# A fused attention and Mish kernel: two more buffers for first-layer results, softmax weights in PSUM, and a new order of steps

## The chip, the core and the metric

The kernel runs on one core of a Trainium2 chip. Its time is the device time in microseconds (us) of one execution; the median of a few executions is quoted. Five engines work side by side, each through its own queue of instructions in a fixed order, and wait for each other through semaphores: TensorE (PE, matrix products, with results in PSUM), VectorE (DVE), ScalarE (ACT), GpSimd (POOL) and SyncE (SP, which here issues the DMA transfers). PSUM has eight banks of 512 fp32 columns by 128 partitions.

## The reference

All inputs are fp32, with S = 2048 rows, D = 640, H = 32 heads of Dh = 20, windows of W = 8 keys with a stride of 2, and F = 1728.

```
x = A_x
g = sigmoid((x * gate_w).sum(-1, keepdims=True))
# a: sliding, dilated, causal attention
q, k, v = split_heads(x @ wqkv)
logits[h, s, w] = q[h, s] . k[h, s - 2 * w] * Dh ** -0.5     # -1e9 where s - 2 * w < 0
o[h, s] = sum_w softmax_w(logits)[h, s, w] * v[h, s - 2 * w]
a = merge_heads(o) @ wo
# b: Dense, Mish, Dense
h = x @ w1 + b1
b = (h * tanh(softplus(h))) @ w2
out = g * a + (1 - g) * b
```

## The kernel before

Every fp32 product is made of three matmuls on split numbers: an operand is cut into a high part (ACT copies it rounded, L444) and a low part (DVE or POOL subtracts, L447), and `mm3` (L510 to L514) multiplies high by high, high by low and low by high into one PSUM group. Halves of the products are combined so that fewer products are needed, at the price of additions of inputs and of partial sums.

The work comes in steps with names. `u.n.i` is group i of a unit n of the projection x @ wqkv (eight units; 0 to 3 are for the first half of the rows, 4 to 7 for the second). Units 2 and 3 are made together: `p.2.j.a1` to `p.2.j.c3` (j = 0 to 3) are the steps of the pair. `q.P.n` is a block of the MLP's first layer (P = 0: half of the rows, in the form with fewer products; P = 1: the same for the other half), in the groups `first`, `second`, `m1` to `m4`, `l1`, `l2`.

In a block `q.0.n`, a group's partial sum is carried on: `seed` (L1144) is an ACT copy from one PSUM bank into the next one or into an `hb` buffer in SBUF, and the next group adds to it. `added` (L1162) is a DVE add of a bank to the kept sum in an `hb` buffer; it also empties the bank. Then `acted` (L1150) is Mish on ACT. First-layer results wait in `hb` buffers, of which there are six, until they are combined (L1017, DVE or POOL) and stored by DMA.

In the pair of units, `c1` (L876 to L882) takes a bank of ring "sb", ACT copies a kept sum into it (L879), PE adds six matmuls, and DVE makes a difference (`sum_to`, L826) in a bank of ring "qb". Then `c2` adds to the first bank and `c3` to the second; both wait for that DVE operation (`self.seeded`), and the results go to the next unit by way of ACT (L680 to L684).

The attention runs on DVE between these operations. For two slots of rows at a time: ACT copies q into `qg` in PSUM (L575), DVE multiplies q by the window of keys (L569, 2560 elements a partition) and reduces (L572) to the logits `lg`. For four slots: DVE takes the maximum `mx` (L590) and subtracts it (L591), ACT takes the exponential (L592) and writes it, multiplied by the gate, into `pw` in SBUF (L596, four pieces), and DVE sums, inverts and multiplies `pw` into `pg` in PSUM (L603 to L605). Then come the products with v (L614, L618).

There are three PSUM banks in a ring "qb", three in a ring "sb", and two that the attention's `pg` and `qg` share. A planner goes through the steps named in a table `ORDER`, adds the other engines' work by costs and ranks, and so fixes the order of the instructions on every engine. What an engine does next is then fixed; the waits decide when.

Of the kernel before, what the change touches and what calls it, by code (L numbers as in the profile page):

```python
# [253 lines left out]
ORDER = """
u.0.5 u.0.7 u.0.4 last.0 u.0.6 q.0.0.first pieces.0.1 q.0.0.m1 q.0.1.first wq.1 pieces.0.2 q.0.1.second q.0.0.second q.0.0.m3 q.0.0.m4 q.0.1.m1 last.1
q.0.0.l2 q.0.0.l1 q.0.0.m2 q.0.1.m3 sum q.0.1.m4 u.1.1 u.1.7 u.1.0 u.1.3 q.0.1.l1 q.0.1.l2 u.1.2 q.0.1.m2 u.1.4 u.1.5 q.0.2.first q.0.2.m1 u.1.6
q.0.2.second q.0.2.m3 q.0.2.m2 wa.2 q.0.2.m4 p.2.1.a1 pieces.0.3 p.2.0.a1 sum p.2.0.a2 q.0.2.l2 p.2.0.a3 p.2.0.b1 p.2.1.a2 q.0.2.l1 p.2.1.a3 p.2.0.b2
p.2.2.a1 p.2.2.a2 p.2.2.a3 p.2.2.b1 p.2.3.a1 p.2.1.b2 p.2.2.b2 p.2.3.a2 pieces.0.4 p.2.1.b1 p.2.3.a3 p.2.3.b1 p.2.3.b2 q.0.3.first q.0.3.m1
q.0.3.second q.0.3.m3 q.0.3.m2 q.0.3.m4 wc.2 q.0.4.second q.0.3.l1 p.2.0.c0 q.0.4.first q.0.3.l2 p.2.1.c0 q.0.4.m1 q.0.4.m3 q.0.4.m4 q.0.4.m2 q.0.4.l2
pieces.0.5 q.0.5.first q.0.4.l1 p.2.3.c0 q.0.5.m1 q.0.5.m4 q.0.5.second x.3.3 q.0.5.m2 x.2.1 x.3.0 p.2.0.c1 p.2.1.c1 x.3.4 p.2.0.c2 q.0.5.m3 p.2.3.c1  # L260
p.2.2.c0 p.2.2.c1 q.0.5.l1 p.2.3.c2 x.2.2 p.2.3.c3 x.3.2 x.2.3 p.2.2.c3 p.2.2.c2 x.3.1 p.2.0.c3 p.2.1.c3 p.2.1.c2 x.2.4 q.0.5.l2 wq.4 x.2.0 third sum
u.4.1 u.4.3 rest.0 pieces.1.0 u.4.5 sum u.4.0 q.1.0.m2 q.1.0.second u.4.6 u.4.2 u.4.4 u.4.7 sum rest.1 wq.5 sum q.1.0.m1 q.1.0.first u.5.0 pieces.1.1
u.5.1 pieces.1.2 sum u.5.4 u.5.2 u.5.7 wq.6 pieces.1.3 u.5.3 q.1.2.second u.5.5 q.1.1.m2 q.1.1.m1 u.5.6 q.1.1.second u.6.6 u.6.4 sum lastw.1 u.6.7
u.6.5 q.1.1.first q.1.2.m2 u.6.2 u.6.1 pieces.1.4 q.1.2.first q.1.3.m1 sum wq.7 u.6.3 q.1.2.m1 pieces.1.5 q.1.3.m2 q.1.3.second u.6.0 q.1.3.first
q.1.4.first last.2 q.1.4.m2 q.1.4.m1 q.1.4.second q.1.5.second u.7.7 u.7.4 u.7.5 last.3 q.1.5.m2 q.1.5.m1 u.7.0 q.1.5.first u.7.6 u.7.1 u.7.2 u.7.3
rest.2 rest.3
# [1696 lines left out]
```

## Time and profile before

| | |
|---|---|
| median of 3 runs | 620.61 us (620.59 to 622.07) |
| profiled execution | 620.5 us, of which the span of the profile is 618.7 us |
| PE busy | 612.1 us, 99% |
| DVE busy | 582.6 us, 94% |
| ACT busy | 364.8 us, 59% |
| POOL busy | 312.2 us, 50% |

The span runs from the first to the last instruction that the profiler saw; 1.8 us of the execution lie around it. Busy shares are means over the whole span. A matmul's shown duration includes its way through the array, so that the pace is read from start to start. Rows of the timeline show an instruction's start and its duration, and in brackets how long its engine had been idle before it and what ended that.

### The profile page before, as it was taken

The numbers are of one execution on the slowest core, as the hardware profiler recorded it, in microseconds if no ns is written. First come the engines' busy times: TensorE is split into PE (matmuls) and PEld (weight loads), VectorE is DVE, ScalarE is ACT, GpSimd is POOL, SyncE is SP. The second block draws the span as 40 slices with busy tenths as digits, with TensorE's granted clock in tenths as the row PEclk, the third lists the DMA queues.
The fourth block names the chain that finished last, engine by engine and source line by source line (L and its number), as shares of the span: only waits on it lengthen the run. The fifth ranks groups of instructions, "written<-read, shape, count | busy, mean of one in ns | idle before, by whom it ended". The sixth has DMA issues, their size and how long they took to land.

```text
span 618.7 us, 9150 instructions
## 1 busy us (share of the span) xinstructions
PE 612.1 (99%) x2719; PEld 508.5 (82%) x2719; DVE 582.6 (94%) x550; ACT 364.8 (59%) x854; POOL 312.2 (50%) x287
## 2 busy tenths in 40 slices
...
GB/s 321 226 223 114 234 251 145 269 240 313 314 297 220 195 256 275 262 250 187 221 228 344 223 123 279 282 204 276 268 242 249 245 175 184 255 275 289 275 89 119
DMA packets 100769, 145.95 MB, mean 236 GB/s; under 512 B 11552, under 2 KB 54560, under 8 KB 100496
## 3 DMA queue, kind: packets, MB, share of 16 engines
...
q8 instruction: 21, 0.34, 0.2%
...
q14 instruction: 28, 0.23, 0.1%
...
## 4 chain that ended last, share of the span: by engine, by line
PE 98%; DMA 0%; DVE 0%; ACT 0%; issue 0%; SPq 0%; DVEq 0%
PE qb L513 20%; PE qb L512 20%; PE qb L514 20%; PE sb L512 12%; PE sb L513 12%; PE sb L514 12%; PE qb L674 1%; DMA raw<-in_wq 0%; PE sb L518 0%; PE qb L519 0%; PE sb L519 0%; PE qb L518 0%; PE sb L674 0%; DVE pair L1740 0%; ACT hb L1150 0%
## 5 line engine op out<-in xcount | busy, mean ns | idle before, releaser
L447 POOL TENSOR_TENSOR pair<-raw,pair 128x512 fp32r<-128x512 f32 (+4 forms) x127 | 156.3, 1250 | 106.4 <-ACT pair L444 61.9
L513 PE MATMUL qb<-pair 128*128 128x512 f32 (+1 forms) x451 | 174.5, 387 | 0.0
L512 PE MATMUL qb<-pair 128*128 128x512 f32 (+1 forms) x451 | 174.5, 387 | 0.0
L514 PE MATMUL qb<-pair 128*128 128x512 f32 (+1 forms) x451 | 174.5, 387 | 0.0
L444 ACT ACTIVATE pair<-raw 128x512 fp32r<-128x512 f32 (+2 forms) x229 | 133.7, 608 | 61.1 <-DMA raw<-actt 19.4
L512 PE MATMUL sb<-pair 128*128 128x512 f32 (+2 forms) x326 | 126.2, 387 | 1.8 <-ACT sb L879 1.8
L513 PE MATMUL sb<-pair 128*128 128x512 f32 (+2 forms) x326 | 126.0, 387 | 0.0
L514 PE MATMUL sb<-pair 128*128 128x512 f32 (+2 forms) x326 | 126.0, 387 | 0.0
L512 PEld LDWEIGHTS qb<-pair 128*128 128x128 f32 x451 | 84.7, 188 | 16.7
L513 PEld LDWEIGHTS qb<-pair 128*128 128x128 f32 x451 | 84.7, 188 | 16.6
L514 PEld LDWEIGHTS qb<-pair 128*128 128x128 f32 x451 | 84.7, 188 | 16.5
L614 DVE TENSOR_TENSOR pr<-kvq,pg 128x1280 f32<-128x1280 f32 x64 | 93.5, 1483 | 0.9
L569 DVE TENSOR_TENSOR pr<-kvq,qg 128x2560 f32<-128x2560 f32 x32 | 89.9, 2809 | 2.0 <-ACT qg L575 0.5
L618 DVE TENSOR_REDUCE kvq<-pr 128x320 f32<-128x2560 f32 x32 | 90.2, 2818 | 0.9
L572 DVE TENSOR_REDUCE lg<-pr 128x128 f32<-128x2560 f32 x32 | 90.2, 2817 | 0.8
L447 DVE TENSOR_TENSOR pair<-raw,pair 128x512 fp32r<-128x512 f32 (+2 forms) x102 | 71.3, 720 | 3.9 <-ACT pair L444 2.3
L512 PEld LDWEIGHTS sb<-pair 128*128 128x128 f32 x326 | 61.2, 188 | 14.8 <-ACT sb L879 2.2
L514 PEld LDWEIGHTS sb<-pair 128*128 128x128 f32 x326 | 61.2, 188 | 12.3
L513 PEld LDWEIGHTS sb<-pair 128*128 128x128 f32 x326 | 61.2, 188 | 12.2
L1017 POOL TENSOR_TENSOR hb<-hb 128x512 f32<-128x512 f32 x34 | 44.3, 1312 | 24.9 <-ACT hb L1150 10.4
L680 ACT ACTIVATE kvq<-qb 128x320 f32<-128x320 f32 x55 | 23.9, 435 | 55.7 <-PE qb L514 55.6
L444 ACT ACTIVATE pair<-hb 128x512 fp32r<-128x512 f32 (+3 forms) x62 | 36.5, 588 | 3.7 <-PE sb L514 2.0
...
## 6 DMA issues: line engine op xcount, KB each, us to landing
...
```

The source lines that it names most:

```text
L444: a = add("ACT", act_ns(n), lambda: A.activation(hi(), raw(), AF.Copy), after, rank=rank, take=take, hold=hold)
L447: return (V if e == "DVE" else G).tensor_tensor(lo(), raw(), hi().bitcast(F32), op=OP.subtract)
L512: nc.tensor.matmul(ps, ah, bh, start=first, stop=False, skip_group_check=more)
L513: nc.tensor.matmul(ps, ah, bl, start=False, stop=False, skip_group_check=more)
L514: nc.tensor.matmul(ps, al, bh, start=False, stop=last, skip_group_check=more)
L569: return V.tensor_tensor(pr, window(kv, s0, 0), qg[:, :, None, :].to_broadcast([128, 2, W, QF]), op=OP.mult)
L572: V.tensor_reduce(lg_w[:, s0:s0 + 2], pr.rearrange("p s w (h d) -> p s w h d", d=DH), op=OP.add, axis=AX.X)
L614: V.tensor_tensor(pairs[:, s].rearrange("p k i (h d) -> p k i h d", d=DH), vw, pg[:, s0 + s].rearrange("p (k i) h -> p k i h", i=2)[:, :, ...
L618: V.tensor_reduce(q[:, s0:s0 + 2], pairs.rearrange("p s k i f -> p s f k i"), op=OP.add, axis=AX.XY)
L674: nc.tensor.matmul(ps.t[:, :n], X[0, kc].t[:, a, i * 128:(i + 1) * 128], WQ[0, kc].t[:, b, :n], start=a == b and kc == 0, stop=False)
L680: a = add("ACT", 330, lambda: A.activation(kv[:, 7 + s], ps.t[:, QF:3 * QF].rearrange("p (a b) -> p a b", a=2), AF.Copy), [done] + before, ...
L1017: return (V if e == "DVE" else G).tensor_tensor(t.t[:, i:i + n], a.t[:, j:j + n], b.t[:, k:k + n], op=op)
```

## The change

There are eight `hb` buffers in place of six. To make room in SBUF, `pw` goes: ACT writes the weighted exponentials straight into `pg` in PSUM, and DVE multiplies them in place. `mx` moves into the tile of `qg`, which is now one whole bank (`qm`). The first buffer for k and v, a row of zeros (`bound`) and the gate's helpers become smaller. A table BANKS names groups that take a bank of the other ring. The table ORDER is new throughout. After the change line numbers in the body are higher by five.

```diff
-NPAIR, NRAW, NH = 24, 8, 6
+NPAIR, NRAW, NH = 24, 8, 8
+BANKS = {'q03al': 's', 'p23be': 'q', 'p22de': 's', 'u47': 's', 'q1211': 's', 'q1301': 'q', 'u43': 's', 'u06': 's', 'q1501': 'q', 'q1300': 's', 'u41': 's', 'u05': 's', 'l2': 's', 'q1411': 's', 'q1401': 'q', 'q1310': 'q', 'q1400': 's', 'q1100': 's', 'l3': 's', 'q1510': 'q', 'q1210': 'q'}
...
-p.2.2.c0 p.2.2.c1 q.0.5.l1 p.2.3.c2 x.2.2 p.2.3.c3 x.3.2 x.2.3 p.2.2.c3 p.2.2.c2 x.3.1 p.2.0.c3 p.2.1.c3 p.2.1.c2 x.2.4 q.0.5.l2 wq.4 x.2.0 third sum
+x.2.1 q.0.5.first x.2.2 x.3.1 q.0.4.l2 p.2.3.c0 x.2.3 q.0.4.l1 q.0.5.second p.2.2.c0 q.0.5.m1 q.0.5.m4 p.2.3.c1 q.0.5.m2 x.2.4 x.3.2 p.2.2.c1 x.3.0
+x.3.3 p.2.0.c1 p.2.3.c2 wq.4 p.2.2.c2 q.0.5.m3 q.0.5.l1 p.2.1.c1 p.2.1.c3 p.2.3.c3 p.2.2.c3 p.2.0.c2 p.2.0.c3 p.2.1.c2 x.2.0 q.0.5.l2 third u.4.3 sum
...
+    def bank_buf(name, ring):
+
+        return sb_buf() if BANKS.get(name, ring) == "s" else qb_buf()
...
-    bound = keep.tile([1, HQ, 7], F32)
+    bound = keep.tile([1, 1, 1], F32)
...
-    pw = at.tile([128, 8, W, HQ], F32, name="pw")
-    pw_h = pw.rearrange("p s w h -> p s h w")
     pg = shared.tile([128, 8, W, HQ], F32, name="pg")
-    qg = shared.tile([128, 2, QF], F32, name="qg")
+    pg_h = pg.rearrange("p s w h -> p s h w")
+    qm = shared.tile([128, 512], F32, name="qg")
+    qg = qm[:, :2 * QF].rearrange("p (s f) -> p s f", f=QF)
     qg_free = [None]
     pr = at.tile([128, 2, W, QF], F32, name="pr")
-    mx = at.tile([128, 8, HQ], F32, name="mx")
+    mx = qm[:, 2 * QF:2 * QF + 8 * HQ].rearrange("p (s h) -> p s h", h=HQ)
...
             def weighted():
                 for i in range(a, a + 4):
-                    A.activation(pw_h[:, i], lg[:, i], AF.Copy, scale=gate[:, P, i:i + 1])
+                    A.activation(pg_h[:, i], lg[:, i], AF.Copy, scale=gate[:, P, i:i + 1])
...
-            return t, step("DVE", 430, lambda: V.tensor_tensor(pg[:, h], pw[:, h], sm[:, h, None, :].to_broadcast([128, 4, W, HQ]), op=OP.mult), [copied])
+            return t, step("DVE", 430, lambda: V.tensor_tensor(pg[:, h], pg[:, h], sm[:, h, None, :].to_broadcast([128, 4, W, HQ]), op=OP.mult), [copied])
...
         def c1(self, j):
-            ga, de, n = sb_buf(), qb_buf(), NCOL
+            ga, de, n = bank_buf(f"p{self.u}{j}ga", "s"), bank_buf(f"p{self.u}{j}de", "q"), NCOL
```

What the new tables do is seen in the instructions. On DVE, ahead of the first difference of the c1 steps, the kernel before has these rows in its queue, from the reduction that follows the add of q.0.4's l1 (L447 are splits, L1162 the adds that empty a bank, L1017 a combination of hb buffers, L826 the differences):

```order
L572 TENSOR_REDUCE lg<-pr 128x2x8x8
L525 STREAM_TRANSPOSE ot<-kvq_269 128x4x5x32
L569 TENSOR_TENSOR pr<-kvq_268,qg 128x2560
L447 TENSOR_TENSOR pair<-raw,pair 128x512 x2
L1017 TENSOR_TENSOR hb<-hb 128x512
L447 TENSOR_TENSOR pair<-raw,pair 128x512
L1162 TENSOR_TENSOR hb<-hb,sb 128x512 x2
L447 TENSOR_TENSOR pair<-raw,pair 128x512
L590 TENSOR_REDUCE mx<-lg 128x32
L591 TENSOR_TENSOR lg<-lg,mx 128x256
L572 TENSOR_REDUCE lg<-pr 128x2x8x8
L826 TENSOR_TENSOR qb<-sb,pair 128x496 x3
```

After the change the same stretch reads as follows, from the add of q.0.4's l1 itself:

```order
L1167 TENSOR_TENSOR hb<-hb,sb 128x512
L574 TENSOR_TENSOR pr<-kvq_268,qg 128x2560
L1022 TENSOR_TENSOR hb<-hb 128x512
L577 TENSOR_REDUCE lg<-pr 128x2x8x8
L530 STREAM_TRANSPOSE ot<-kvq_269 128x4x5x32
L574 TENSOR_TENSOR pr<-kvq_268,qg 128x2560
L1167 TENSOR_TENSOR hb<-hb,sb 128x512 x2
L595 TENSOR_REDUCE qg<-lg 128x32
L452 TENSOR_TENSOR pair<-raw,pair 128x512
L596 TENSOR_TENSOR lg<-lg,qg 128x256
L577 TENSOR_REDUCE lg<-pr 128x2x8x8
L831 TENSOR_TENSOR qb<-sb,pair 128x496
```

Three of the four splits have left this stretch, and a second multiplication (L574) has come into it; two differences (L831) follow here in place of three. On ACT, around the copies of the c1 steps (L879), the kernel before has:

```order
L444 ACTIVATE pair<-raw 128x512 x3
L575 ACTIVATE qg<-kvq_268 128x320
L444 ACTIVATE pair<-raw 128x512
L1144 ACTIVATE hb<-qb 128x512
L1150 ACTIVATE hb<-qb,bias 128x512
L444 ACTIVATE pair<-raw 128x512
L1150 ACTIVATE hb<-sb,bias 128x512
L879 ACTIVATE sb<-pair 128x496 x3
L1150 ACTIVATE hb<-hb,bias 128x512 x2
L592 ACT_TABLE_LOAD
```

After the change ACT has there:

```order
L449 ACTIVATE pair<-raw 128x512 x3
L1155 ACTIVATE hb<-qb,bias 128x512
L580 ACTIVATE qg<-kvq_268 128x320
L449 ACTIVATE pair<-raw 128x512
L884 ACTIVATE sb<-pair 128x496
L1155 ACTIVATE hb<-hb,bias 128x512
L884 ACTIVATE sb<-pair 128x496
L1155 ACTIVATE hb<-hb,bias 128x512
L1155 ACTIVATE hb<-sb,bias 128x512
L597 ACT_TABLE_LOAD
```

Three c1 copies in a row have become two, with a Mish between them. Directly behind, with the waits shown, the queue before goes on with the exponential, the four weighted pieces (L596) and the evacuation of the first c2 result (L680):

```order
L592 ACT_TABLE_LOAD
L592 ACTIVATE lg<-lg 128x256 [waits DVE_49]
L596 ACTIVATE pw<-lg,gate 128x8x8 [waits Activation_49]
L596 ACTIVATE pw<-lg,gate 128x8x8 x3
L680 ACTIVATE kvq_269<-sb 128x320 [waits PE_49]
```

After the change it goes on with these rows, as far as the third c1 copy:

```order
L597 ACT_TABLE_LOAD [waits DVE_49]
L597 ACTIVATE lg<-lg 128x256 [waits Activation_49]
L601 ACTIVATE pg<-lg,gate 128x8x8 [waits Activation_49] x4
L685 ACTIVATE kvq_269<-sb 128x320 [waits PE_49]
L687 ACTIVATE kvq_269<-sb 128x160
L689 ACTIVATE hx<-sb 128x16
L449 ACTIVATE pair<-raw 128x512 [waits DMAHW3_49,DMAHW0_49,DVE_49]
L884 ACTIVATE sb<-pair 128x496 [waits Activation_49]
```

Each of the four weighted pieces now waits for the ACT instruction ahead of it, where before only the first did, and the third c1 copy comes behind the evacuation of the first c2 result.

## Rows read from the trace of the kernel before

**Rows 1.** The page, part 1: busy us, share of the span, instructions.

```profile
PE 612.1 (99%) x2719; PEld 508.5 (82%) x2719; DVE 582.6 (94%) x550; ACT 364.8 (59%) x854; POOL 312.2 (50%) x287
```

**Rows 2.** Windows: length, busy us of each engine, granted clock, DMA share, GB/s.

```profile
20.00:160.00 140.00, 140.00 (x626) 117.19 (x625) 135.50 (x105) 93.64 (x228) 102.54 (x91) 1.00 0.73 226
160.00:180.00 20.00, 18.23 (x80) 14.68 (x79) 19.88 (x19) 17.62 (x38) 13.42 (x11) 1.00 0.96 315
180.00:600.00 420.00, 420.00 (x1865) 349.95 (x1865) 402.00 (x388) 238.10 (x558) 191.07 (x176) 1.00 0.81 238
```

**Rows 3.** Waits of PE: us in total, times, longest.

```profile
PE sb L512 <- ACT sb L879: 1.8, 1, 1.8
```

**Rows 4.** Timeline of PE, 159 to 178: start us, duration us, instruction, idle before.

```profile
160.01 0.39 PE L514 MATMUL sb<-pair 128*128 128x512 f32 x1
...
170.89 0.39 PE L514 MATMUL sb<-kvq,pair 128*128 128x512 f32 x1
173.06 0.49 PE L512 MATMUL sb<-pair 128*128 128x496 f32 x1 [1.77 <-ACT sb L879]
...
174.50 0.39 PE L512 MATMUL sb<-pair 128*128 128x496 f32 x1
...
175.84 0.39 PE L512 MATMUL sb<-pair 128*128 128x496 f32 x1
...
177.25 0.49 PE L512 MATMUL sb<-pair 128*128 128x496 f32 x1
```

**Rows 5.** Timeline of DVE, 159 to 178.

```profile
161.80 0.68 DVE L1162 TENSOR_TENSOR hb<-hb,sb 128x512 f32<-128x512 f32 x1
162.40 2.81 DVE L572 TENSOR_REDUCE lg<-pr 128x128 f32<-128x2560 f32 x1
165.13 0.83 DVE L525 STREAM_TRANSPOSE ot<-kvq 128x640 f32<-128x640 f32 x1
165.88 2.78 DVE L569 TENSOR_TENSOR pr<-kvq,qg 128x2560 f32<-128x2560 f32 x1
168.59 1.31 DVE L447 TENSOR_TENSOR pair<-raw,pair 128x512 fp32r<-128x512 f32 x2
169.83 0.68 DVE L1017 TENSOR_TENSOR hb<-hb 128x512 f32<-128x512 f32 x1
170.43 0.68 DVE L447 TENSOR_TENSOR pair<-raw,pair 128x512 fp32r<-128x512 f32 x1
171.03 1.45 DVE L1162 TENSOR_TENSOR hb<-hb,sb 128x512 f32<-128x512 f32 x2
172.40 0.68 DVE L447 TENSOR_TENSOR pair<-raw,pair 128x512 fp32r<-128x512 f32 x1
173.00 0.41 DVE L590 TENSOR_REDUCE mx<-lg 128x32 f32<-128x256 f32 x1
173.45 0.42 DVE L591 TENSOR_TENSOR lg<-lg,mx 128x256 f32<-128x256 f32 x1
173.79 2.81 DVE L572 TENSOR_REDUCE lg<-pr 128x128 f32<-128x2560 f32 x1
176.52 1.83 DVE L826 TENSOR_TENSOR qb<-sb,pair 128x496 f32<-128x496 f32 x3
```

**Rows 6.** Timeline of ACT, 168 to 178.

```profile
169.03 0.43 ACT L575 ACTIVATE qg<-kvq 128x320 f32<-128x320 f32 x1
...
171.32 0.63 ACT L444 ACTIVATE pair<-raw 128x512 fp32r<-128x512 f32 x1 [0.24 <-PE sb L514]
...
172.43 1.59 ACT L879 ACTIVATE sb<-pair 128x496 f32<-128x496 f32 x3
...
177.03 1.14 ACT L596 ACTIVATE pw<-lg,gate 128x64 f32<-128x64 f32 x4
```

**Rows 7.** Groups of DVE by line and shape: count, busy us, mean ns.

```profile
L447 DVE TENSOR_TENSOR pair<-hb,pair 128x512 fp32r<-128x512 f32 x30 | 20.4, 682 | 0.0
...
L826 DVE TENSOR_TENSOR sb<-qb,hb 128x496 f32<-128x496 f32 x4 | 2.7, 667 | 0.0
```

More of the change, by code (lines that the diff above doesn't have):

```diff
@@ L253 @@
 C_PAIR = True
+BANKS = {'q03al': 's', 'p23be': 'q', 'p22de': 's', 'u47': 's', 'q1211': 's', 'q1301': 'q', 'u43': 's', 'u06': 's', 'q1501': 'q', 'q1300': 's', 'u41': 's', 'u05': 's', 'l2': 's', 'q1411': 's', 'q1401': 'q', 'q1310': 'q', 'q1400': 's', 'q1100': 's', 'l3': 's', 'q1510': 'q', 'q1210': 'q'}
 ORDER = """
-u.0.5 u.0.7 u.0.4 last.0 u.0.6 q.0.0.first pieces.0.1 q.0.0.m1 q.0.1.first wq.1 pieces.0.2 q.0.1.second q.0.0.second q.0.0.m3 q.0.0.m4 q.0.1.m1 last.1
-q.0.0.l2 q.0.0.l1 q.0.0.m2 q.0.1.m3 sum q.0.1.m4 u.1.1 u.1.7 u.1.0 u.1.3 q.0.1.l1 q.0.1.l2 u.1.2 q.0.1.m2 u.1.4 u.1.5 q.0.2.first q.0.2.m1 u.1.6
@@ L257 @@
[L257 to L260, printed above, removed]
@@ L261 @@
-p.2.2.c0 p.2.2.c1 q.0.5.l1 p.2.3.c2 x.2.2 p.2.3.c3 x.3.2 x.2.3 p.2.2.c3 p.2.2.c2 x.3.1 p.2.0.c3 p.2.1.c3 p.2.1.c2 x.2.4 q.0.5.l2 wq.4 x.2.0 third sum
-u.4.1 u.4.3 rest.0 pieces.1.0 u.4.5 sum u.4.0 q.1.0.m2 q.1.0.second u.4.6 u.4.2 u.4.4 u.4.7 sum rest.1 wq.5 sum q.1.0.m1 q.1.0.first u.5.0 pieces.1.1
-u.5.1 pieces.1.2 sum u.5.4 u.5.2 u.5.7 wq.6 pieces.1.3 u.5.3 q.1.2.second u.5.5 q.1.1.m2 q.1.1.m1 u.5.6 q.1.1.second u.6.6 u.6.4 sum lastw.1 u.6.7
-u.6.5 q.1.1.first q.1.2.m2 u.6.2 u.6.1 pieces.1.4 q.1.2.first q.1.3.m1 sum wq.7 u.6.3 q.1.2.m1 pieces.1.5 q.1.3.m2 q.1.3.second u.6.0 q.1.3.first
@@ L265 @@
-q.1.4.first last.2 q.1.4.m2 q.1.4.m1 q.1.4.second q.1.5.second u.7.7 u.7.4 u.7.5 last.3 q.1.5.m2 q.1.5.m1 u.7.0 q.1.5.first u.7.6 u.7.1 u.7.2 u.7.3
-rest.2 rest.3
+u.0.5 u.0.7 last.0 u.0.6 u.0.4 q.0.0.first pieces.0.1 q.0.1.first q.0.0.second q.0.0.m1 q.0.0.m3 q.0.0.m4 q.0.1.second q.0.1.m1 q.0.0.m2 q.0.1.m4
+q.0.1.m3 wq.1 last.1 q.0.0.l2 q.0.1.l2 u.1.1 q.0.0.l1 u.1.0 u.1.2 q.0.1.m2 u.1.3 u.1.4 u.1.7 pieces.0.2 q.0.1.l1 sum u.1.5 q.0.2.first q.0.2.m1 u.1.6
+q.0.2.second q.0.2.m3 wa.2 p.2.1.a1 p.2.0.a1 q.0.2.m4 p.2.0.a2 pieces.0.3 sum q.0.2.m2 q.0.2.l2 p.2.1.a2 p.2.0.a3 p.2.0.b2 p.2.0.b1 p.2.1.a3 q.0.2.l1
@@ new lines @@
+p.2.2.a1 p.2.1.b1 p.2.2.a2 p.2.2.a3 p.2.2.b2 pieces.0.4 p.2.1.b2 p.2.3.a1 p.2.3.a2 p.2.2.b1 p.2.3.b1 p.2.3.a3 p.2.1.c0 wc.2 p.2.3.b2 x.3.4 q.0.3.first
+p.2.0.c0 q.0.3.m1 q.0.3.second q.0.3.m3 q.0.3.m4 q.0.4.second q.0.3.l1 q.0.3.m2 q.0.4.first q.0.4.m1 q.0.3.l2 q.0.4.m4 q.0.4.m2 q.0.4.m3 pieces.0.5
+x.2.1 q.0.5.first x.2.2 x.3.1 q.0.4.l2 p.2.3.c0 x.2.3 q.0.4.l1 q.0.5.second p.2.2.c0 q.0.5.m1 q.0.5.m4 p.2.3.c1 q.0.5.m2 x.2.4 x.3.2 p.2.2.c1 x.3.0
+x.3.3 p.2.0.c1 p.2.3.c2 wq.4 p.2.2.c2 q.0.5.m3 q.0.5.l1 p.2.1.c1 p.2.1.c3 p.2.3.c3 p.2.2.c3 p.2.0.c2 p.2.0.c3 p.2.1.c2 x.2.0 q.0.5.l2 third u.4.3 sum
@@ new lines @@
+rest.0 pieces.1.0 u.4.0 rest.1 u.4.5 u.4.1 sum q.1.0.m2 u.4.6 u.4.2 u.4.4 sum u.4.7 wq.5 q.1.0.m1 sum q.1.0.second pieces.1.1 pieces.1.2 q.1.0.first
+u.5.2 u.5.0 u.5.4 u.5.1 sum wq.6 pieces.1.3 u.5.7 q.1.2.second q.1.1.m2 u.5.5 u.5.3 u.5.6 q.1.1.second q.1.2.first sum u.6.3 q.1.1.m1 u.6.4
+q.1.1.first u.6.2 u.6.7 u.6.5 q.1.2.m2 q.1.3.m2 u.6.1 q.1.3.m1 q.1.2.m1 lastw.1 u.6.6 u.6.0 pieces.1.4 sum last.2 wq.7 pieces.1.5 q.1.3.second
+q.1.4.m1 u.7.5 q.1.4.first q.1.4.m2 q.1.4.second q.1.5.second last.3 q.1.3.first u.7.0 u.7.7 u.7.4 q.1.5.m2 q.1.5.m1 q.1.5.first u.7.6 u.7.2 u.7.1
@@ L267 @@
+u.7.3 rest.2 rest.3
 """
@@ L376 @@
     bias = top.tile([128, 120], F32, name="bias")
-    bound = keep.tile([1, HQ, 7], F32)
+    bound = keep.tile([1, 1, 1], F32)
     zt = keep.tile([128, 2, 8], F32)
     gate = keep.tile([128, 2, 8], F32)
-    gc = keep.tile([128, 2, 32], F32)
-    gt = keep.tile([128, 2, 32], F32)
+    gc = keep.tile([128, 32], F32)
+    gt = keep.tile([128, 32], F32)
     hx = keep.tile([128, 2, 8, NQ, RQ], F32)
@@ L398 @@
     g_d = [dram.tile([8, 128], F32, name=f"g{P}") for P in range(2)]
-    kvq = [at.tile([128, 2 * KC * D], F32, name="kvq0"), pe.tile([128, 15 * ROW + 8 * QF], F32, name="kvq1"),
+    kvq = [at.tile([128, 6144], F32, name="kvq0"), pe.tile([128, 15 * ROW + 8 * QF], F32, name="kvq1"),
            pe.tile([128, 6, 2, 512], F32R, name="kvq2")]
```

38 lines of the change are left out of this document (19 added, 19 removed).

## The prediction

> **What bounds the kernel now.** I began with the page's busy times: TensorE (PE) is busy for 612.1 of 618.7 us, VectorE (DVE) for 582.6, and ScalarE (ACT) and GpSimd (POOL) lie far below [rows 1]. PE does the same 2719 matmuls after the change, so its order can only move the time in which it stands still. The windows say where that is [rows 2]: in 20:160 and 180:600 PE is busy from end to end, 160:180 lacks 1.77 us, the granted clock is 1.00 in all three, and the rest lies in the head and the tail, which the change leaves as they are. The waits of PE name one stop inside the kernel, 1.8 us for the copy of L879 [rows 3]. So everything that can be won is in this one place, and everything else that can happen is a new stop.
>
> PE's timeline shows the place [rows 4]. The l2 group of q.0.5 ends with the matmul that starts at 170.89. Start to start, 512 columns take 0.227 us ((170.89 - 160.01) / 48) and 496 columns 0.223 ((175.84 - 174.50) / 6). Three c1 groups of six matmuls follow, then the first c2 group. Without a stop c1 would begin at 170.89 + 0.23 = 171.12, and c2 at 171.12 + 18 x 0.223 = 175.13. They begin at 173.06 and 177.25. The second start is the one that counts, and it is **2.12 us** late: 1.94 at c1, the rest at c2, which shows in no row of waits.
>
> Who is late is read on DVE's timeline [rows 5]. c1 needs a bank that DVE's adds (L1162, from 171.03) must have emptied, then the copy on ACT, which starts at 172.43 [rows 6]. c2 needs the sum of L826 that starts at 176.52; PE starts 0.73 later. From the add of q.0.4 at 161.80 to this sum DVE works 14.72 us without a gap. So DVE's queue sets both starts in this stage, though PE is the busy engine.
>
> **The change part by part.** *The deciding stretch.* Nothing about PE's groups between q.0.5.second and the end of l2 changes in number: 48 matmuls from the end of q.0.4's l1 to 171.12 [rows 4]. Two things move. First, only two c1 groups now stand ahead of the first c2 (on ACT the copy for the third comes behind the evacuation of c2's result). PE would like to start c2 at 171.12 + 12 x 0.223 = **173.80**, 1.33 earlier than before. Second, DVE's queue in front of the first sum is another. It begins again with the add of q.0.4's l1. I let that start at 160.5: its matmuls end at 160.01 + 0.39 = 160.40 [rows 4], and DVE comes to it earlier, because from the end of q.0.4's m3 PE has 18 matmuls to do (18 x 0.227 = 4.09 us) and DVE one add and one reduction (0.60 + 2.73 = 3.33), so up to 0.7 us of lateness from further back is swallowed here.
>
> Behind it stand, by the start-to-start times of rows 5: this add 0.60, multiplication 2.71, hb product 0.60, reduction 2.73, transpose 0.75, multiplication 2.71, two adds 1.37, max 0.45, one split 0.60, subtraction 0.34, reduction 2.73. The sum is **15.59**, against 14.72 before: three splits (1.84) are gone and one multiplication (2.71) has come in. The sum of L831 thus starts at 160.5 + 15.59 = 176.09, and c2 at 176.09 + 0.73 = 176.82. That is 176.82 - 173.80 = **3.02 us** late, 0.90 more than the 2.12 of now. In a word: the sum comes 0.4 earlier, PE asks for it 1.3 earlier.
>
> It makes no difference to this that c1 itself waits less. The first of the two adds starts at 160.5 + 10.10 = 170.6; the qg copy comes after the multiplication, 170.7 to 171.1, a split follows to 171.7, then the first c1 copy; PE follows 0.63 behind a copy's start (173.06 - 172.43), so at 172.3. c2 could start at 172.3 + 2.68 + 0.11 for the slow first matmul (the six from 173.06 take 1.44, the six from 174.50 take 1.34), 175.1, and waits 1.7 more for the sum. That the c1 copies now have Mish between them costs nothing within these 1.7 us. What is late next are the remaining c1, c2 and c3 groups. DVE has then one hb product, a multiplication and a reduction ahead of its next sum: 176.09 + 2 x 0.67 + 0.60 + 2.71 + 2.73 = 183.5. By the order of the steps PE asks for it after c2 and c3 of two units and two more c1 groups, near 185, so that I see no third stop here.
>
> *Two more hb buffers.* They remove waits for a free buffer. PE had none behind such a wait [rows 3]. Zero; what they pay is already in the order.
>
> *Softmax weights in PSUM, in place.* ACT writes four pieces into pg. Before they overlap, four in 1.14 us [rows 6]; now each has a wait for the one before it. Bounds: nothing, or four one behind the other, each at most as long as the larger qg copy, 0.43: 4 x 0.43 - 1.14 = 0.58 us for each of 16 times, 9.3 us on ACT. I take the upper end, since the waits stand in the order. ACT is idle for 41% of the span and PE's evacuations are a few us ahead in most stages, so on the path it costs nothing; in the deciding stretch it stands behind both c1 copies. If that cover fails for one evacuation, the price is 0.58 once.
>
> *Max and subtraction on an operand in PSUM.* No row has these with PSUM. The nearest: an add of 496 columns from PSUM takes 667 ns, a split of 512 from SBUF 682 [rows 7]. If all of a split's time went by columns, 16 of them would be 21 ns, and PSUM would cost 6 more; if none did, PSUM would be 15 cheaper. I take zero; two such operations in the stretch make less than 0.03 us either way. [...]
>
> *Smaller constants, the bank table.* A broadcast in place of a stored zero row on ACT, the same number of instructions: zero. The banks of the other ring change who must have emptied a bank, not how many there are; the cost is zero unless a new wait comes of it, which is a case below.
>
> **Sum.** The profiled run took 620.5 us, 1.8 more than its span of 618.7; with 3.02 - 2.12 = 0.90 it would take 621.4. The median of the runs shown lies 0.1 higher, 620.61, so the forecast is 620.61 + 0.90 = **621.5 us**.
>
> **Rivals.** *A shared tile makes max wait (slower).* mx now lies in the tile of qg. DVE's max must wait for ACT's qg copy, which had its own tile before. It comes to it at 160.5 + 11.47 = 171.97, and the copy ends at 171.1 by my working, 0.87 ahead. But ACT is busy 5 us in 5 around here (no idle before the copy at 169.03, 0.24 in all to 173.95 [rows 6]), and three splits and a Mish stand in front. Every us beyond 0.87 is a us at c2. From a copy that ends at 172.95 on, the kernel is slower by 0.3%; four operations late (three splits and a Mish, taken at the split's 0.63 each, 2.5) give 621.5 + 2.5 - 0.87 = 623.1. For it: the full queue. Against: now ACT takes up its copy 0.37 us after DVE's multiplication released it (165.88 + 2.78 = 168.66, and 169.03), with three splits just as near ahead of it. [...]
>
> *No gain, no loss.* If DVE keeps the pace but runs 0.9 us shorter than my sum (one split's place and the 0.1 at the start), the stops are as long as before: 620.6.
>
> *The stops vanish (faster).* 620.61 - 2.12 = 618.5. It would need the sum 3 us earlier, more than a whole reduction; nothing in DVE's queue allows it, unless two of the long operations fall behind the sums.
>
> *A stop elsewhere.* Seeds on ACT, which carry a partial sum from bank to bank, have six matmuls of cover (1.36 us) where their group follows at once, and take about 0.6 like the copies at 172.43 [rows 6]; the new order has places where the seed stands behind a DVE add, as at m4 of q.0.1. A miss costs 0.5 to 1.5 us: 622.0 to 623.0. For it: DVE is 94% busy. Against: before, no such stop shows in 20:160 [rows 2].
>
> **How the numbers follow.** Within 0.3% means 1.86 us, about what a measurement of this kernel can tell. Two stops of 3.0 together: 0.55, with an own range of 621.0 to 622.3. As before: 0.15. Vanish: 0.06. Late max: 0.13; stop elsewhere: 0.11, half of it beyond 622.47. Faster 0.06, slower 0.21 (all of late max, half of the stop elsewhere, and 0.02 from the likeliest's upper edge), same 0.73. The range of 620.3 to 623.0 leaves out the vanished stops and the far ends of the two slow cases.
>
> **What would show it.** In the changed trace: c1 near 172.3, c2 near 176.8 with a visible wait of about 1.7 us for the sum of L831; the sum at 176.1; no other wait of PE between 20 and 600; DVE's max at about 172.0 with no idle time before it. Wrong would be: a sum before 175 (then DVE's queue was read wrongly), an idle DVE before the max, or a PE wait outside 170:178.

## The result, and the profile after

The changed kernel takes **622.08 us** (median of 16 runs, 621.81 to 622.59), the kernel before 620.89 (16 runs beside it, 620.26 to 622.07): a ratio of **1.0019**, 95% interval 1.0011 to 1.0027. So 1.2 us more, where 0.9 more was forecast (621.5). By the prediction's bound of 0.3% this is no change that counts, but it is a loss that can be measured.

Of the 71 executions of the kernel before that stand beside the experiments, 15 have a mean granted clock of 0.996 or 0.997 and took 0.6 to 1.8 us more than the median of the others, while all 16 of the changed kernel are at 0.998 or more; the ratios take in all executions, and so differ by up to 0.0008 from the ratios of the medians.

The busy times after, as in [rows 1]; the span is 620.5 us, the execution 622.3:

```profile
PE 612.1 (99%) x2719; PEld 508.2 (82%) x2719; DVE 581.3 (94%) x548; ACT 373.8 (60%) x858; POOL 315.4 (51%) x289
```

PE is busy for the same 612.1 us. The windows as in [rows 2], and the waits of PE as in [rows 3] (us in total, times, longest):

```profile
20.00:160.00 140.00, 139.54 (x623) 116.64 (x622) 133.33 (x105) 96.34 (x231) 103.09 (x92) 1.00 0.73 226
160.00:180.00 20.00, 17.48 (x76) 13.94 (x76) 19.91 (x17) 17.31 (x37) 15.95 (x13) 1.00 0.95 313
```

```profile
PE sb L517 <- DVE qb L831: 1.3, 1, 1.3
PE sb L517 <- ACT sb L884: 1.2, 1, 1.2
...
PE qb L679 <- DVE kvq L1752: 0.7, 1, 0.7
PE sb L517 <- ACT sb L1149: 0.5, 1, 0.5
```

PE now lacks 2.52 us in 160:180, where it lacked 1.77, and 0.46 in 20:160, where it lacked nothing. One stop has become two in the deciding stage (L884, L831), and a small one for a seed (L1149) has come. The row of L1752 is the head of the kernel, its first loads. It was 0.2 before, and over the twelve profiles of this study it is between nothing and 0.7 whatever the kernel, so that it is scatter; here it moves all later times by 0.5. The two stages on PE's timeline, as in [rows 4]:

```profile
61.41 0.39 PE L519 MATMUL qb<-kvq,pair 128*128 128x512 f32 x1
62.26 0.50 PE L517 MATMUL sb<-pair 128*128 128x512 f32 x1 [0.46 <-ACT sb L1149]
...
172.06 0.39 PE L519 MATMUL sb<-kvq,pair 128*128 128x512 f32 x1
173.65 0.49 PE L517 MATMUL sb<-pair 128*128 128x496 f32 x1 [1.20 <-ACT sb L884]
...
177.92 0.50 PE L517 MATMUL sb<-pair 128*128 128x496 f32 x1 [1.33 <-DVE qb L831]
```

At 61.41 + 0.23 = 61.64 PE was free and went on at 62.26. In the deciding stage l2 ends at 172.06 + 0.23 = 172.29; c1 starts at 173.65, 1.36 late, and c2 at 177.92. Without a stop c2 would start at 172.29 + 12 x 0.223 = 174.97. It is **2.95 us** late; the forecast was 3.02. DVE's queue, as in [rows 5]:

```profile
161.72 0.68 DVE L1167 TENSOR_TENSOR hb<-hb,sb 128x512 f32<-128x512 f32 x1
...
171.84 1.45 DVE L1167 TENSOR_TENSOR hb<-hb,sb 128x512 f32<-128x512 f32 x2
173.21 0.42 DVE L595 TENSOR_REDUCE qg<-lg 128x32 f32<-128x256 f32 x1
...
174.47 2.81 DVE L577 TENSOR_REDUCE lg<-pr 128x128 f32<-128x2560 f32 x1
177.20 0.67 DVE L831 TENSOR_TENSOR qb<-sb,pair 128x496 f32<-128x496 f32 x1
```

From the add of q.0.4's l1 to the first difference there are 177.20 - 161.72 = **15.48 us**; 15.59 was forecast. PE starts 0.72 behind the difference, as before. ACT, as in [rows 6]:

```profile
171.24 0.67 ACT L1155 ACTIVATE hb<-qb,bias 128x512 f32<-128x512 f32 x1
171.95 0.44 ACT L580 ACTIVATE qg<-kvq 128x320 f32<-128x320 f32 x1
172.49 0.63 ACT L449 ACTIVATE pair<-raw 128x512 fp32r<-128x512 f32 x1
173.03 0.57 ACT L884 ACTIVATE sb<-pair 128x496 f32<-128x496 f32 x1
...
177.70 1.37 ACT L601 ACTIVATE pg<-lg,gate 128x64 f32<-128x64 f32 x4
```

From 171.24 to the c1 copy at 173.03 each operation begins within 0.1 us of the end of the one before it. But the split at 172.49 also follows the end of PE's last l2 matmul, 172.06 + 0.39 = 172.45, and so does the split in the kernel before (170.89 + 0.39 = 171.28, the split at 171.32, ACT idle until PE released it [rows 6]). The c1 copy stands behind this split in both; experiment 6 tells the two reasons apart. The four weighted pieces take 1.37 us and not 1.14 each time: 0.23 more, with their waits and with the result in PSUM in place of SBUF (one piece by itself takes 0.32 and not 0.41, by the medians of the 64). The upper bound of 0.58 was too high by more than half. For the operations with PSUM (DVE by line and shape; first the subtraction in the kernel before, then subtraction and max after the change):

```profile
L591 DVE TENSOR_TENSOR lg<-lg,mx 128x256 f32<-128x256 f32 x16 | 7.4, 463 | 0.4
```

```profile
L596 DVE TENSOR_TENSOR lg<-lg,qg 128x256 f32<-128x256 f32 x16 | 6.7, 420 | 1.0 <-ACT qg L580 0.5
L595 DVE TENSOR_REDUCE qg<-lg 128x32 f32<-128x256 f32 x16 | 6.7, 420 | 1.0 <-ACT lg L587 0.7
```

420 ns both. The 463 of before is a mean with one subtraction of 1073 ns in it; the other 15, with all operands in SBUF, take 410 to 427, 422 in the mean. So nothing is paid for the subtraction's operand in PSUM, which agrees with the zero that was taken. Max, whose result now lies in PSUM, takes 420 where it took 409 (L590, the mean of 16): 0.01 us, within the 0.03 that was allowed for the two.

So, on PE's clock from the head on: 0.74 more for the seed (0.62 late, and a first matmul of 0.34 in place of 0.23), and 2.95 in place of 2.12 in the deciding stage, 0.83 more. That is 1.57. From the fourth product matmul (5.83 before, 6.37 after), where the head is over, to the start of the last one (614.53 and 616.34) it is 608.70 and 609.97, a difference of 1.27. The stops thus make 0.3 more than the whole difference. This 0.3 lies in the kernel before: a slow first matmul at 67.77 (0.33 to the next start, 0.11 too much), and the pace behind its stage, where from 177.6 to 189.2 the matmuls of 496 columns follow each other at 0.223 us and in the changed kernel from 178.3 to 191.0 at 0.220 (0.16 over 52 of them). Experiment 2 shows the two paces again.

### The profile page after: what moved, and what is told of

The parts are those of the page before. It is cut to its first block, busy times and chain, and to the rows that moved or that the text cites. A ratio compares the mean times of both kernels' runs of the same rounds, so it can differ in the third digit from the quotient of the medians.

```text
span 620.5 us, 9136 instructions
## 1 busy us (share of the span) xinstructions
PE 612.1 (99%) x2719; PEld 508.2 (82%) x2719; DVE 581.3 (94%) x548; ACT 373.8 (60%) x858; POOL 315.4 (51%) x289
## 4 chain that ended last, share of the span: by engine, by line
PE 71%; DVE 1%; issue 0%; DVEq 0%
PE qb L517 14%; PE qb L518 14%; PE qb L519 14%; PE sb L517 10%; PE sb L518 10%; PE sb L519 10%; DVE lg L577 0%; PE qb L523 0%; PE sb L524 0%; PE sb L523 0%; PE qb L524 0%; DVE qb L831 0%; DVE qg L595 0%; DVE kvq L1671 0%; DVE lg L596 0%
## 5 line engine op out<-in xcount | busy, mean ns | idle before, releaser
L452 POOL TENSOR_TENSOR pair<-raw,pair 128x512 fp32r<-128x512 f32 (+3 forms) x129 | 160.2, 1259 | 93.5 <-ACT pair L449 58.0
L517 PE MATMUL qb<-pair 128*128 128x512 f32 (+1 forms) x426 | 164.7, 387 | 0.0
L518 PE MATMUL qb<-pair 128*128 128x512 f32 (+1 forms) x426 | 164.7, 387 | 0.0
L519 PE MATMUL qb<-pair 128*128 128x512 f32 (+1 forms) x426 | 164.7, 387 | 0.0
L517 PE MATMUL sb<-pair 128*128 128x512 f32 (+2 forms) x351 | 136.1, 388 | 3.0 <-DVE qb L831 1.3
L518 PE MATMUL sb<-pair 128*128 128x512 f32 (+2 forms) x351 | 135.8, 387 | 0.0
L519 PE MATMUL sb<-pair 128*128 128x512 f32 (+2 forms) x351 | 135.7, 387 | 0.0
L574 DVE TENSOR_TENSOR pr<-kvq,qg 128x2560 f32<-128x2560 f32 x32 | 90.0, 2812 | 3.5 <-ACT qg L580 2.0
L517 PEld LDWEIGHTS qb<-pair 128*128 128x128 f32 x426 | 80.0, 188 | 15.7
L519 PEld LDWEIGHTS qb<-pair 128*128 128x128 f32 x426 | 79.9, 188 | 15.6
L518 PEld LDWEIGHTS qb<-pair 128*128 128x128 f32 x426 | 79.9, 188 | 15.6
L517 PEld LDWEIGHTS sb<-pair 128*128 128x128 f32 x351 | 65.9, 188 | 17.4 <-DVE qb L831 1.7
L519 PEld LDWEIGHTS sb<-pair 128*128 128x128 f32 x351 | 65.9, 188 | 13.3
L518 PEld LDWEIGHTS sb<-pair 128*128 128x128 f32 x351 | 65.9, 188 | 13.1
L452 DVE TENSOR_TENSOR pair<-raw,pair 128x512 fp32r<-128x512 f32 (+3 forms) x100 | 67.3, 696 | 3.3 <-ACT pair L449 3.3
L1022 POOL TENSOR_TENSOR hb<-hb 128x512 f32<-128x512 f32 x37 | 47.9, 1305 | 28.2 <-ACT hb L1155 12.8
L685 ACT ACTIVATE kvq<-qb 128x320 f32<-128x320 f32 x50 | 21.9, 439 | 54.1 <-PE qb L519 53.9
```

The source lines that it names most:

```text
L452: return (V if e == "DVE" else G).tensor_tensor(lo(), raw(), hi().bitcast(F32), op=OP.subtract)
L517: nc.tensor.matmul(ps, ah, bh, start=first, stop=False, skip_group_check=more)
L518: nc.tensor.matmul(ps, ah, bl, start=False, stop=False, skip_group_check=more)
L519: nc.tensor.matmul(ps, al, bh, start=False, stop=last, skip_group_check=more)
L574: return V.tensor_tensor(pr, window(kv, s0, 0), qg[:, :, None, :].to_broadcast([128, 2, W, QF]), op=OP.mult)
L685: a = add("ACT", 330, lambda: A.activation(kv[:, 7 + s], ps.t[:, QF:3 * QF].rearrange("p (a b) -> p a b", a=2), AF.Copy), [done] + before, ...
```

## Experiments

In most of them an operation is only moved. To do this without touching the rest, the planner keeps its plan, and an operation listed in HOLD is issued at a later place of the plan, behind the one that it is listed with:

```diff
+    def emit(self, t, e):
+        if t.i in HOLD:
+            self.held.append(t)
+            return None
+        ins = t.fn(e) if t.both else t.fn()
+        for h in [h for h in self.held if HOLD[h.i] == t.i]:
+            self.held.remove(h)
...
-                    ins = t.fn(e) if t.both else t.fn()
+                    ins = self.emit(t, e)
```

**1. The layout alone.** The changed kernel with six buffers and the old order:

```diff
-NPAIR, NRAW, NH = 24, 8, 8
+NPAIR, NRAW, NH = 24, 8, 6
-BANKS = {'q03al': 's', ...}
+BANKS = {}
```

> The changed kernel's memory layout (weights in PSUM, in place; max in the tile of qg; smaller constants) with six buffers, without the bank table and with the order of steps of before, so that every engine's queue reads as in the kernel before. Theory P (place): the layout costs nothing by itself, and all of the 1.2 us come from where PE has to stop in the new order. Then 620.9 us, a ratio of 1.000 within its interval, and PE's only stop is the old one at c1 and c2. Rival L (layout): the weights, written one behind the other, and the max behind the qg copy delay evacuations; then most of the 1.2 us are here too, 621.7 to 622.1 (ratio 1.0013 to 1.0019), and ACT or DVE is idle before a max or a weighted piece ahead of a new stop of PE.

Measured: 620.77 us (12 runs), ratio 1.0002 (0.9990 to 1.0013). PE's only stop behind the head is the old one:

```profile
PE sb L517 <- ACT sb L884: 1.8, 1, 1.8
```

The profiled execution took 623.0, 2.2 above the median of its runs. The excess is in the head: eight of its first product matmuls follow each other at 0.43 us in place of 0.23. From the matmul at 18.18 to the last it needs 598.84 us, and the kernel before, from the same matmul by count at 15.84, 598.68. Theory L falls: weights and max in PSUM cost 0.16 us at most in these profiles. The difference lies in the new order with its two more buffers and its bank table, which no run takes apart.

**2. The seed.** `HOLD = {203: 293}`: one multiplication goes behind the add of q.0.0's l1.

> The changed kernel with one DVE operation moved: the multiplication ahead of the add of q.0.0's l1 now comes behind that add, so that the seed of q.0.1's m4 on ACT is not held up. Theory P: PE's stop of 0.74 us at 62.3 goes and nothing takes its place: 621.4 us, ratio 1.0008. Rival H (the head: what the profile shows there, 0.5 us, is what the medians show): the stop at 62.3 goes, but DVE's lateness gives it back later, 622.1, ratio 1.0019.

Measured: 621.83 us (11 runs), ratio 1.0009 (1.0001 to 1.0018), between 621.4 and 622.1 by the median and at theory P by the ratio. The traces show more. On DVE the add no longer stands behind the multiplication; the engine is idle until PE is through with its matmuls:

```profile
59.34 0.69 DVE L1180 TENSOR_TENSOR hb<-hb,sb 128x512 f32<-128x512 f32 x1 [1.72 <-PE sb L532]
```

The stop of PE at 62 is gone. Two matmuls of this run, and then the same two in the changed kernel:

```profile
61.41 0.39 PE L531 MATMUL sb<-pair 128*128 128x512 f32 x1
...
148.07 0.39 PE L531 MATMUL sb<-pair 128*128 128x512 f32 x1
```

```profile
62.60 0.40 PE L518 MATMUL sb<-pair 128*128 128x512 f32 x1
...
148.72 0.39 PE L518 MATMUL sb<-pair 128*128 128x512 f32 x1
```

Each matmul here has its like in the changed kernel, by count: this run is 1.19 ahead after the seed (61.41 and 62.60), 0.65 at 148, and 0.44 from 194 on. At 60.5, ahead of the seed, it had been 0.45 ahead by its shorter head, and it ends 0.44 ahead. So in these two profiles all of the 0.74 is given back; the runs leave room for a gain, since the ratio is 0.0010 below that of the changed kernel, with intervals that overlap. In the profile 0.2 goes back at 108 (a first matmul after a short wait for DVE), and 0.6 without any stop: between 108 and 133, and again between 178 and 191, the matmuls of 496 columns follow each other at 0.223 us here and at 0.220 in the changed kernel. The rival had the right end by the profile, and not the right way: most of the loss is not DVE's lateness.

**3. One reduction moved.** `HOLD = {659: 794}`: it goes behind the first two differences.

> The changed kernel with one reduction on DVE (2.73 us) moved from ahead of the first two differences of the c1 steps to behind them. Theory P: the second stop (c2 of p.2.3, 1.5 us) goes, since the differences then follow c1's matmuls at once; but the reduction now stands, with the multiplication and the next reduction, ahead of the difference of p.2.0, which comes 2.3 us too late for its c2. So 622.08 - 1.47 + 2.33 = 622.9 us, ratio 1.0032, with the stop at c2 of p.2.0 near 187. Rival (DVE has slack behind the stage): no third stop, 620.6, ratio 0.9995.

Measured: 624.17 us (6 runs, three of them 622.9 to 623.7 at a mean granted clock of 0.999 or 1.000, three 624.6 to 625.1 at 0.996 or 0.997), ratio 1.0045 (1.0028 to 1.0062). PE's longest wait and DVE's queue:

```profile
PE sb L530 <- DVE qb L844: 2.3, 1, 2.3
```

```profile
174.85 0.68 DVE L844 TENSOR_TENSOR qb<-sb,pair 128x496 f32<-128x496 f32 x1 [0.74 <-PE sb L532]
176.25 0.68 DVE L844 TENSOR_TENSOR sb<-sb,pair 128x496 f32<-128x496 f32 x1 [0.72 <-PE sb L532]
...
185.75 0.67 DVE L844 TENSOR_TENSOR qb<-sb,pair 128x496 f32<-128x496 f32 x1
```

The differences now follow c1 at once (DVE waits for PE ahead of both), c2 no longer stops, and the difference of p.2.0 at 185.75 comes 2.3 us too late, behind the reduction that was moved, a product, a multiplication and the next reduction, as worked out. The executions at the higher clock are near the 622.9 forecast. What was not forecast is a wait for ACT (L702) at 256.52: it and the slow matmul behind it cost another 0.5.

**4. Two reductions moved.** `HOLD = {659: 794, 662: 835, 663: 835}`.

> As the run with one reduction moved, and the next reduction too, behind the differences of p.2.0 and p.2.1 (with the ACT writes to its result that follow it). Theory P: the second stop goes and the third does not come, 622.08 - 1.47 = 620.6 us, ratio 0.9995. What could come is a stop before u.4.3 for the split of x.2.0, which now lies behind the reduction: up to 0.8 us, 621.4, ratio 1.0008. Rival (the lateness is only pushed along, stop for stop): 622.1 or more.

Measured: 625.57 us (5 runs), ratio 1.0072 (1.0057 to 1.0086): a miss by 5 us for theory P, and inside the open end of the rival. The place, ahead of u.4.3, had been named, at up to 0.8 us. PE's longest wait, and what ACT did ahead of the split that PE waited for:

```profile
PE sb L530 <- ACT pair L462: 2.3, 1, 2.3
```

```profile
190.09 0.62 ACT L600 ACTIVATE lg<-bound 1x56 f32<-1x56 f32 x4 [5.97 <-DVE lg L590]
```

The writes of L600 wait for the reduction and stand in ACT's queue ahead of the splits that PE needs for u.4.3. Moving a step had moved what is queued behind it. Two more costs are new: an hb product on DVE beside two splits on POOL, and PE's clock after the stop (window: length, busy us of PE, PEld, DVE, ACT, POOL, granted clock, DMA share, GB/s):

```profile
183.41 3.33 DVE L1035 TENSOR_TENSOR hb<-hb 128x512 f32<-128x512 f32 x1
```

```profile
183.39 1.55 POOL L465 TENSOR_TENSOR pair<-raw,pair 128x512 fp32r<-128x512 f32 x1
```

```profile
193.00:194.00 1.00, 1.00 (x3) 0.51 (x2) 0.96 (x3) 0.96 (x5) 0.00 (x0) 0.50 0.00 0
```

The product is most of the miss. It holds up the difference of p.2.1 behind it, for which PE stops by 0.75 at 187.40, and the reduction behind that, for which L600 waits. With the 0.68 us that the same product takes in the changed kernel (at 185.44), all of this would come 2.66 us earlier: an estimate from these rows is no stop at 187.40, and one of 0.7 ahead of u.4.3, as theory P had it, in place of 2.5, with the low clock behind it.

**5. The reduction left out.** Two slots of logits aren't reduced:

```diff
             def red():
+                if (u, P, s0) == (2, 0, 2):
+                    return
```

> The changed kernel without one reduction on DVE: the one of 2.73 us ahead of the first difference of the c1 steps is left out, and two slots of logits with it; nothing else moves. Theory Q (DVE's queue is full from about 60 us on, so that its work up to a place sets when the place is reached; moving work only moves the stop): with the work gone, not moved, the second stop of PE goes and none comes back: 622.08 - 1.47 = 620.6 us, ratio 0.9995, where the run with the same reduction moved was slower by 2 us. Rival (c2 waits for something else than DVE's backlog, a bank or a load): the stop stays, 622.1.

Measured: 621.50 us (11 runs), ratio 1.0001 (0.9992 to 1.0010), 0.0018 below the changed kernel's (0.0013 by the medians). c2's stop is gone, so that the backlog on DVE it was. But a stop of 0.8 came for the difference of p.2.0 (DVE, then POOL):

```profile
174.80 0.68 DVE L833 TENSOR_TENSOR qb<-sb,pair 128x496 f32<-128x496 f32 x1 [0.75 <-PE sb L519]
176.20 0.68 DVE L833 TENSOR_TENSOR sb<-sb,pair 128x496 f32<-128x496 f32 x1 [0.72 <-PE sb L519]
176.79 1.74 DVE L1024 TENSOR_TENSOR hb<-hb 128x512 f32<-128x512 f32 x1
...
184.03 0.67 DVE L833 TENSOR_TENSOR qb<-sb,pair 128x496 f32<-128x496 f32 x1
```

```profile
174.18 3.80 POOL L452 TENSOR_TENSOR pair<-raw,pair 128x512 fp32r<-128x512 f32 x3 [1.41 <-DMA o<-ot]
```

DVE idles for 0.75 and 0.72 ahead of the first two differences, since PE has not got further, and is then late for the third. Of 1.47 won, 0.9 is lost again. The rows show why: the hb product at 176.79 runs into the last of three splits on POOL (to 177.98) and takes 1.74 us, where in the changed kernel the same product, at 178.36, takes 0.68. An estimate from these rows: with 0.68 the difference would start 1.07 earlier, at 182.96, and PE, 0.73 behind it and busy until 183.98, would not have stopped. So theory Q fails by this product; that DVE's work can't be done ahead of time here is not shown.

**6. An earlier reduction left out.** The same with `(2, 0, 4)`: it stands ahead of the two adds.

> The changed kernel without the reduction that stands ahead of the two adds of q.0.5 on DVE, so that the adds and all behind them come 2.73 us earlier. If DVE's queue sets both stops, as the prediction has it, c1 starts 1.2 us earlier too, and both stops go: 622.08 - 2.7 = 619.4 us, ratio 0.9976. Rival (ACT sets the first stop: its three splits, Mish, the qg copy and a split fill its queue to within 0.1 us of the c1 copy): c1 starts at most 0.2 us earlier, and only the second stop goes: 620.5, ratio 0.9994.

Measured: 621.61 us (11 runs), ratio 1.0008 (1.0000 to 1.0017), where the rival had 620.5. c1's stop is the same 1.36 to 0.01 us: DVE does not set it. PE, DVE and ACT:

```profile
171.39 0.39 PE L519 MATMUL sb<-kvq,pair 128*128 128x512 f32 x1
172.98 0.49 PE L517 MATMUL sb<-pair 128*128 128x496 f32 x1 [1.20 <-ACT sb L886]
```

```profile
169.16 1.47 DVE L1169 TENSOR_TENSOR hb<-hb,sb 128x512 f32<-128x512 f32 x2 [0.64 <-ACT ot L639]
171.39 0.43 DVE L597 TENSOR_REDUCE qg<-lg 128x32 f32<-128x256 f32 x1 [0.77 <-ACT qg L582]
172.48 0.69 DVE L452 TENSOR_TENSOR pair<-raw,pair 128x512 fp32r<-128x512 f32 x1 [0.67 <-DMA actt<-hb]
```

```profile
171.82 0.63 ACT L449 ACTIVATE pair<-raw 128x512 fp32r<-128x512 f32 x1 [0.46 <-PE sb L519]
```

Nor does the length of ACT's queue set it, as the rival had it: ACT idles for 0.46 ahead of the split at 171.82, until PE's last l2 matmul is through (171.39 + 0.39 = 171.78), and the c1 copy stands behind this split. From the start of that matmul to the start of c1 it takes 1.58 or 1.59 us in all six profiles of the new order that have the split there, whatever DVE does; 2.16 in the kernel before and in experiments 1 and 7, where Mish of l2 stands between too; and 1.12 and 1.79 in experiments 9 and 10, which move the split. PE's first stop is thus a relay: PE ends l2, ACT splits, ACT copies, PE goes on.

Of 2.73 us taken from DVE, 2.1 turn up as idle time: 0.64 ahead of the first add, 0.77 in which the max waits for the qg copy of the shared tile (the rival of the prediction, seen here at last), and 0.67 ahead of the low half of wq.4's split, whose high half on ACT ends at 172.45 by this relay (the DMA that the row names is not the last wait). Only 0.4 of the second stop goes.

**7. The same reduction left out of the kernel before**, `(2, 0, 2)`.

> The kernel before without the reduction that stands ahead of its first difference (the same two slots of logits). In that kernel c1 is late for what lies ahead of this reduction, and PE has three c1 groups to do behind it, which end at 177.2 without any wait for the difference. So the 2.73 us less on DVE should gain nothing: 620.8 us, ratio 0.9999. If the difference were what sets c2 there, as the prediction has it, c2 would begin earlier: but by no more than 0.1 us. A gain above 0.5 us would mean that DVE's backlog is paid for at another place in the kernel before.

Measured: 620.83 us (11 runs), ratio 0.9994 (0.9985 to 1.0003). No gain, as forecast: DVE waits for PE ahead of the differences instead,

```profile
175.62 0.68 DVE L828 TENSOR_TENSOR qb<-sb,pair 128x496 f32<-128x496 f32 x1 [0.83 <-PE sb L514]
```

and c2 starts when the third c1 group is through. So in the kernel before even the second start is hardly DVE's: 1.94 of the 2.12 at c2 are late at c1 already, and 0.11 is the slow first matmul of c1.

**8. The buffers with the old order.** `NH = 8`, `BANKS = {}` and the old ORDER.

> The changed layout and eight buffers with the order of steps of before and without the bank table: the buffers alone. The planner now puts one difference ahead of a multiplication and a reduction on DVE and three behind them, and the exponential ahead of the second c1 copy on ACT. By the durations of the kernel before, the second c1 copy then starts near 176.9 (now 172.9), the first c2 near 180.2 (now 177.3) and the second c2 another 1.1 later than that: 3 to 4.5 us more, 624 to 625.4, ratio 1.005 to 1.007. Rival (buffers remove waits and can only help): 620.9 or less.

Measured: 626.34 us (4 runs), ratio 1.0085 (1.0071 to 1.0099), above the 624 to 625.4 expected. The stops in the stage are at the places worked out (the second c1 copy starts at 177.55, 176.9 was expected), and they are followed by a lower clock (0.50 in 178 to 180), as in experiment 4, and by stops of 1.1 and 0.4 us near 330, which were not in the estimate:

```profile
PE sb L517 <- ACT sb L884: 2.4, 1, 2.4
PE sb L517 <- DVE qb L831: 1.5, 1, 1.5
```

More buffers let the planner start other work earlier on DVE and ACT, and the old order doesn't fit it. With the new order eight buffers cost far less; the new order with six was not run.

**9. A cure for the changed kernel.** `HOLD = {809: 835, 810: 835, 638: 783, 639: 783, 640: 783}`.

> The changed kernel with five operations moved: the first split of wq.4 (ACT 0.63 us and DVE 0.60 us), which stood ahead of the c1 copies and of the first difference, goes behind all four differences, and the max, the subtraction and the exponential go behind the first difference. Theory R (the first stop is ACT's queue, the second DVE's backlog, and what is moved here is not needed until u.4.3): c1 starts 0.5 us earlier, with the end of the first add; the first difference follows the reduction at once, c2 is 0.7 us late instead of 1.5; the difference of p.2.0 comes just in time. 622.08 - 1.24 = 620.85 us, ratio 0.9999, no more than 0.3 us from the kernel before. Rival (the stops come back further on, near 185 or 256, as when a reduction was moved): 621.5 or more.

Measured: 621.54 us (11 runs), ratio 1.0006 (0.9997 to 1.0015), an interval that holds the forecast's 0.9999 and the rival's 1.0010 alike. The two stops shrink as forecast, by 0.47 and 0.79, and a third comes, because the exponential, now later, holds up ACT ahead of the next c1 copies:

```profile
175.95 0.49 PE L530 MATMUL sb<-pair 128*128 128x496 f32 x1 [0.52 <-DVE qb L844]
...
183.50 0.49 PE L530 MATMUL sb<-pair 128*128 128x496 f32 x1 [0.33 <-ACT sb L897]
```

```profile
176.76 1.28 ACT L610 ACT_TABLE_LOAD   x1 [1.90 <-DVE lg L609]
```

Between the same two matmuls it needs 609.65 us where the changed kernel needed 609.97: of 1.26 won in the stage, 0.9 is lost in its second half, as the rival had it.

**10. The same cure for the kernel before.** `HOLD = {914: 794, 915: 794}`: the first split of wq.4 goes behind three differences.

> The kernel before with the same split of wq.4 moved behind the first three differences, on ACT and on DVE. Theory R: c1 starts after Mish of l2 and its own copy, 0.5 us earlier than now, and the difference, 0.6 us earlier, is there in time: 620.89 - 0.5 = 620.4 us, ratio 0.9992, faster than both kernels. Rival (DVE's adds set c1 in the kernel before, as the prediction has it): the adds are where they were, c1 starts no earlier, ratio 1.0000.

Measured: **620.14 us** (11 runs, 619.90 to 621.43), ratio **0.9984** (0.9976 to 0.9993): faster than both kernels, by 0.16% of the kernel before. In its profile (618.9 us, an execution of 620.69, above its median) c1 is 0.37 earlier, and then the adds wait for a store out of an hb buffer:

```profile
172.75 0.50 PE L525 MATMUL sb<-pair 128*128 128x496 f32 x1 [1.40 <-ACT sb L892]
...
177.30 0.49 PE L525 MATMUL sb<-pair 128*128 128x496 f32 x1 [0.30 <-DVE qb L839]
```

```profile
171.67 1.47 DVE L1175 TENSOR_TENSOR hb<-hb,sb 128x512 f32<-128x512 f32 x2 [0.49 <-DMA actt<-hb]
```

The copy for c1 starts at 172.75 - 0.63 = 172.1, before the first of the two adds is through (171.67 + 0.7), so that the adds don't set it; the rival falls. But the profile shows no gain: c2 starts where it did, and from the fourth product matmul to the last it needs 608.82 us, the kernel before 608.70. Where the executions that took 620.14 and less gain their time is not shown; whether they lack this wait of 0.49 was not seen. A part of the ratio is that of the 21 executions of the kernel before beside it five have a mean granted clock of 0.996 or 0.997, and none of these 11 is below 0.999: against the other 16 its mean is 0.65 us less, 0.10%.

## Why the prediction was right

*The deciding stretch.* Right by its own steps: DVE's queue was put at 15.59 us and measured 15.48; c2's lateness at 3.02, measured 2.95; max at 171.97, with the copy 0.87 ahead of it; measured, with the later head and seed, 173.21 and 173.21 - (171.95 + 0.44) = 0.82. Experiments 3 and 5 bear out that DVE's backlog sets the second stop, and experiment 7 that the kernel before doesn't have it. The wait that shows at c2 was put at 1.7 us and is 1.5, since c1 starts 0.18 later against l2 than was worked out: the split ahead of its copy could not start at 171.1, before PE's last l2 matmul was through.

*That DVE sets both starts* was wrong for c1 in both kernels, and for c2 in the kernel before. c1 waits for the relay from PE's last l2 matmul through the split on ACT: experiment 6 took 2.73 us from DVE and the stop stayed, and experiments 9 and 10, which move the split, shorten it. In the kernel before c2 is late because c1 is, but for some 0.1 (experiment 7). DVE sets the second start after the change alone. It didn't hurt the sum, because the 2.12 that was subtracted was read off PE's timeline, whatever set it, and because after the change only the second start counts.

*The stop elsewhere* was listed at m4 of q.0.1, with 0.5 to 1.5 us, as a case for 0.11. It is there with 0.74, outside 170:178, which by the prediction's own list was a sign of being wrong, and the measured 622.08 lies in this case's range as well as in that of the two stops. Removed, it gave nothing in the profile of experiment 2, and at most some 0.6 by the runs. So the sum without it was right by luck in part: 0.83 in the stage, and 0.74 for the seed less the 0.3 that the kernel before loses elsewhere, make the 1.27 of the profiles.

*The late max* did not happen; its mechanism exists (0.77 us in experiment 6). *The stops vanish* and *no gain, no loss* are excluded by the trace; what the latter was said to need, one split's place and 0.1, adds up to 0.7 and not to 0.9. *Buffers at zero* is not shown by itself, since the new order was not run with six; with the old order they cost some 5 us (experiment 8). *Weights in PSUM*, zero on the path: right (experiment 1).

What stays open: why the 496-column matmuls of experiment 2 follow each other at 0.223 us over 25 us and in the changed kernel at 0.220. A stop ahead of them does not decide it: in the kernel before they keep 0.220 from 108 to 132 with no stop since the head but the 0.11 at 67.77, and behind the second stop of the stage, 1.7 us from start to start in both, the pace is 0.223 in experiment 2 and 0.220 in the changed kernel.
